# The value product of 8 of 12 column blocks through Strassen's seven quarter products, two of its four multiplications on GpSimd, in a new order

## The chip, the cores and the metric

The kernel runs on one core of one Trainium2 chip. The core has TensorE (PE: matmuls, and PEld, its weight loads), VectorE (DVE), ScalarE (ACT), GpSimd (POOL) and SyncE (SP), which here issues the DMAs. Each engine takes its instructions in the order of its own queue and waits on semaphores for the others. The metric is the device time of one execution in microseconds (us).

## The reference

The inputs are q, k and v (8 batches, 8 heads, 576 positions, head size 64) and three weights. First comes a retention layer, a causal attention whose scores are multiplied by a decay instead of going through a softmax; its output, 4608 tokens of 512 values, is x. Then comes a gated feed-forward layer of width 1536:

```python
ret = (q @ k.T / sqrt(64)) * Dmat          # Dmat[i, j] = gamma_h ** (i - j) for i >= j, else 0
x = (ret @ v) rearranged to (4608, 512)
gate = 1 / (1 + exp(-(x @ w_gate)))        # 512 x 1536
val = x @ w_val                            # 512 x 1536
out = (gate * val) @ w_out                 # 1536 x 512
```

Inputs and output are float32; the kernel's matmuls take bf16 and sum in float32.

## The kernel before, in words

**Blocks.** The tokens are taken in blocks of 512, 256, 384, 384 and then six of 512 (t0 = 1536 to 4096). While the feed-forward layer of one block runs, the retention layer makes the x of the next one: its steps ("slots", `slot_of_two`) are put between the pieces of the feed-forward work by the loop at the end of the kernel, so the order on every engine is written out by hand; no scheduler moves an instruction.

**Strassen.** In the 512-token blocks a 2-by-2 product of quarters is made from 7 quarter products instead of 8. The 12 column blocks (128 wide) of the gate make 3 units of 4 blocks; a unit is the product of a 2-by-2 arrangement of weight quarters (two halves of the 512 inner rows, two pairs of column blocks) and of x quarters (two halves of the inner rows, two halves of 256 tokens). One quarter product is `product`: 4 matmuls of 256 columns. A direct column block (`value`) is 4 matmuls of 512 columns. The step g16 is unit 1's product 6 of the gate, v4 the direct value product of column block 4. The sums of the weights (`wgt_sb`) are made once, in the blocks of 384 tokens; the sums of x (`xsum`) for each block by GpSimd.

**A gate unit's evictions.** The products gather in three PSUM banks, a, g and e. After product 1 ScalarE copies a to g; product 2 is added into g and ScalarE takes the sigmoid of g. After 6 ScalarE copies a to SBUF (u2), after 5 it copies e (s5). After 3 VectorE adds e to u2, after 7 it adds a to s5, and ScalarE takes the sigmoids of both; after 4 ScalarE takes that of a. The sigmoids go to `gv`. `settle` puts the last two sigmoids behind the matmuls of the following step. A direct value block is one VectorE multiplication, gv times the PSUM bank.

**Output part.** `quarters` makes gv @ w_out with Strassen again, from gv and its sums `gsum` (per unit: third_sum on GpSimd, the others on VectorE; for unit 2 all four on GpSimd, for each pair of column blocks). Between its products stand two retention slots in every 512-token block but the last. In a slot (`slot_of_two`) PE makes the values of two steps (`val`), VectorE then reads one element of each bank (`glance`), PE makes the scores and products of two new steps, and then the second part of `val`, which goes to the banks that glance has read. Products 1 and 2 of the next block's first gate unit (`gates_early`) stand at the end of the output part; the first 512-token block has no such place ahead of it and starts with g01 and g02.

**Order and room.** `ORDER` is the list of steps of a 512-token block, with the sums that stand behind a step after a colon. PSUM has eight banks: tr, pv and st one each, qk two, and a ring of three (`ffn_psum`). Finished output tiles wait in `stores` until more than KEEP are there, then the oldest leaves on SP's queue. GpSimd's other work is the casting of q, k and v (`casts_to`), which SP then transposes by DMA.

Of the kernel before, what the change touches and what calls it, by code (L numbers as in the profile page):

```python
# [16 lines left out]
def kernel(  # L17
# [32 lines left out]
    osb_pool = ctx.enter_context(tc.tile_pool(name="osb", bufs=13))  # L50
# [4 lines left out]
    sum_pool = ctx.enter_context(tc.tile_pool(name="sum", bufs=5))  # L55
# [26 lines left out]
    ffn_psum = Ring(3)  # L82

# [174 lines left out]
    sbd = [(consts if i else lead).tile([P, M, P], BF16, name=f"sbd{i}") for i in range(4)]  # L258
# [43 lines left out]
    wgt_sb = consts.tile([P, 3, NU, 2, 2 * P], BF16)  # L302

    def wg_quarters(u):

        fa, fb = (slice((4 * u + 2 * y) * P, (4 * u + 2 * y + 2) * P) for y in range(2))
        return wg_sb[:, 0:2, fa], wg_sb[:, 2:4, fa], wg_sb[:, 0:2, fb], wg_sb[:, 2:4, fb]

    def wg_sums(i, u):

        a11, a12, a21, a22 = wg_quarters(u)
        s1, s2, s4 = (wgt_sb[:, j, u] for j in range(3))
        to, a, b, op = ((s1, a21, a22, ALU.add), (s2, s1, a11, ALU.subtract), (a21, a11, a21, ALU.subtract),
                        (s4, a12, s2, ALU.subtract))[i]
        nc.vector.tensor_tensor(out=to, in0=a, in1=b, op=op)
# [202 lines left out]
    def third_out(apart):  # L518

        ps = pair_ps[5][0][0]  # L520
        share = nat_pool.tile([P, 2, P], FP32, tag="apart", name="apart", bufs=1)
        nc.vector.tensor_copy(out=share, in_=apart)
        cols = slice(5 * P, 6 * P)
        nc.vector.tensor_tensor(out=x_out(slice(0, 2), cols), in0=x_in(ps[:, 0:2], cols), in1=x_in(share, cols), op=ALU.add)
        nc.scalar.copy(out=x_out(slice(2, 4), cols), in_=x_in(ps[:, 2:4], cols))
# [188 lines left out]
    def leave_share(s, j):  # L714

        if before(s, j) is not None:
            shares[s, j] = nat_pool.tile([P, 2, 64], FP32, tag="share", name=f"share_{s}_{j}", bufs=4)
            nc.scalar.copy(out=shares[s, j], in_=val_ps[s][1 - j][:, M:M + 2])
# [140 lines left out]
    KEEP = 9  # L859
# [59 lines left out]
    def gate_units(gvs, t0):  # L919

        units = []
        banks = [(tr_psum, "tr", pv_psum, "pv", qk_psum, "qk"), (qk_psum, "qk", ffn_psum, "ffn", st_psum, "st"),
                 (pv_psum, "pv", st_psum, "st", tr_psum, "tr")]
# [6 lines left out]
        def bank(u, i, name):  # L930
            pool, tag = banks[u][2 * i:2 * i + 2]
            more = {"written": True} if pool is ffn_psum and name == "g" else {}
            return pool.tile([P, 2, 256], FP32, tag=tag, name=f"gate{name}_{t0}_{u}", **more)

        def keep(u, name, ps):
            t = sum_pool.tile([P, 2, 256], FP32, tag="sum", name=f"gate{name}_{t0}_{u}")
            nc.scalar.copy(out=t, in_=ps)
            return t
# [7 lines left out]
        def left(u, i):  # L946
            a11, a12, a21, a22 = wg_quarters(u)
            return (a11, a12, wgt_sb[:, 2, u], a22, wgt_sb[:, 0, u], wgt_sb[:, 1, u], a21)[i - 1]

        def product(u, i, ps, first):  # L950
            w, x = left(u, i), right(i)
            for f in range(2):
                for kc in range(2):
                    nc.tensor.matmul(ps[:, f], lhsT=w[:, kc, f * P:(f + 1) * P], rhs=x[:, kc],  # L954
                                     start=(first and f == 0 and kc == 0), stop=(f == 1 and kc == 1),
                                     skip_group_check=True)

        of = [{} for _ in range(NU)]

        def gate(u, i):  # L960

            me = of[u]
            if i == 1:
                gv_tile(gvs, t0, 4 * u)
                me["unit"] = made[t0, u]
                me["a"] = bank(u, 0, "a")
            if i == 5:
                me["e"] = bank(u, 2, "e")
            a, e = me["a"], me.get("e")
            product(u, i, {1: a, 6: a, 7: a, 4: a, 5: e, 3: e, 2: me.get("g")}[i], i in (1, 5))  # L970
            settle()

            def sigmoid(r, h, src):
                nc.scalar.activation(out=me["unit"][:, 2 * r:2 * r + 2, h * 256:(h + 1) * 256], in_=src, func=AF.Sigmoid)  # L974

            if i == 1:
                me["g"] = bank(u, 1, "g")
                nc.scalar.copy(out=me["g"], in_=a)
            elif i == 2:
                sigmoid(0, 0, me["g"])  # L980
            elif i == 5:
                me["s5"] = keep(u, "s5", e)
            elif i == 6:
                me["u2"] = keep(u, "u2", a)
            elif i == 3:
                nc.vector.tensor_tensor(out=me["u2"], in0=e, in1=me["u2"], op=ALU.add)  # L986
                waiting.append(lambda: sigmoid(0, 1, me["u2"]))
            elif i == 7:
                nc.vector.tensor_tensor(out=me["s5"], in0=a, in1=me["s5"], op=ALU.add)
                waiting.append(lambda: sigmoid(1, 1, me["s5"]))  # L990
            else:
                sigmoid(1, 0, a)
            return 4 * 256

        def value(fc):

            ps = ffn_psum.tile([P, 512], FP32, tag="ffn", name=f"h2_{t0}_{fc}")
            for kc in range(NKC):
# [6 lines left out]
        return gate, value  # L1005

    EARLY = "g01 g02"
    ORDER = ("g05 g06 g11 g03 g07 g12 g15 v0 g04 v1 g16 v2 g13 v3 g17 g21 v4:00 g14 v5:01:02 g22 g25 v6 g26 g23 v7 "
             "g27 v8 v9:10:2 g24 v10 v11:11:12:2")
    begun = {}  # L1010

    def gates_early(t0):

        gvs = {}
        gate, value = gate_units(gvs, t0)
        begun[t0] = gvs, gate, value
        for x in EARLY.split():
            yield gate(int(x[1]), int(x[2]))

    def quarters(gvs, sums, t0, k):  # L1020
# [42 lines left out]
        def keep(name, ps):  # L1063
            kept[name] = sum_pool.tile([P, 2, W], FP32, tag="sum", name=f"s{name}_{t0}")[:, 0:k]
# [91 lines left out]

    def ffn_units(t0, n, nxt):
        if n < 512:
# [3 lines left out]
            return  # L1162
        if t0 not in begun:
            for cols in gates_early(t0):
                yield cols
        gvs, gate, value = begun[t0]
        sums = []
        for x in ORDER.split():
            if x[0] == "g":
                yield gate(int(x[1]), int(x[2]))  # L1170
                continue
            x, *behind = x.split(":")
            fc = int(x[1:])
            cols = value(fc)
            u = fc // 4
            if fc % 4 == 0:
                sums.append(pair_sums(t0, u))
            if u < NU - 1 and fc % 4 == 3:
                third_sum(made[t0, u], sums[u], slice(0, 2))
            for one in behind:  # L1180
                if len(one) == 2:
                    gv_sum(made[t0, int(one[0])], sums[int(one[0])], slice(0, 2), int(one[1]), nc.vector)
                    continue
                pair = slice(fc % 4 // 2, fc % 4 // 2 + 1)
                for i in range(2):
                    gv_sum(made[t0, u], sums[u], pair, i, nc.gpsimd)
                third_sum(made[t0, u], sums[u], pair)
                gv_sum(made[t0, u], sums[u], pair, 2, nc.gpsimd)
# [225 lines left out]
    for w, (t0, n) in enumerate(BLOCKS):  # L1414
# [6 lines left out]
        if n == 512:  # L1421
            n_h = len(ORDER.split()) + (0 if t0 in begun else len(EARLY.split()))
# [11 lines left out]
        for i, cols in enumerate(ffn_units(t0, n, nxt)):  # L1434
            if w in (1, 2) and i % 2 == 0 and i < 18:
                which, part = (0, 1, 3)[i // 2 % 3], i // 6
                if w == 1:
                    wg_sums(which, part)
                else:
                    wo_sums(which, part, 3)  # L1440
            if w == 2 and n_h <= i < n_h + NU:
                wg_sums(2, i - n_h)
# [53 lines left out]
```

## Time and profile before

| | us |
|---|---|
| median of 3 runs | 317.99 (317.87 to 318.19) |
| the profiled execution | 318.03 |
| its span | 316.3 |
| PE busy | 307.6 |
| VectorE / ScalarE / GpSimd busy | 210.4 / 169.7 / 177.1 |
| gate-and-value part of a 512-token block (five of the six) | 18.89 to 18.90 |
| the same in the first, with g01 and g02 | 20.65 |

The profile is one execution. PE's rows overlap, since matmuls are pipelined: the distance from one row's start to the next one's is what a step costs. The "gate-and-value part" goes from the first product of `ORDER` (g05) to the first product of the output part (qa), read from TensorE's timeline.

### The profile page before, as it was taken

What the parts mean: (1) busy time and instruction counts of PE and PEld (TensorE: products, weight loads), DVE (VectorE), ACT (ScalarE), POOL (GpSimd) and SP (SyncE); (2) the same over time, 40 slices, a digit from 0 to 9 for tenths busy, and PEclk for the clock granted to TensorE, in tenths of its full rate; (3) what the DMA queues carried; (4) which work ended last, traced back from release to release, by engine and by line L of the source; (5) the groups of instructions that cost most, each with busy time, mean ns of one, the idle gap of its engine ahead of it and who ended that gap; (6) DMA issues with size and microseconds to landing.
All of it is one profiled execution on the core that took longest, in us unless ns stands there. A gap on an engine that the chain in (4) does not pass through costs nothing. (4 is left out here: it accounts for less than half of the span.)

```text
span 316.3 us, 9821 instructions
## 1 busy us (share of the span) xinstructions
PE 307.6 (97%) x4038; PEld 210.7 (67%) x4038; DVE 210.4 (67%) x478; ACT 169.7 (54%) x374; POOL 177.1 (56%) x238
## 2 busy tenths in 40 slices
PE   7999999999999998999999999999999999999994
PEld 6664557856545655668866786678667866786683
DVE  6955656778826775688568955885689558826843
ACT  6855555555434337554665476537654765446530
POOL 5784545544644834119981899189918921841170
PEclk9999999999999999999999999999999999999999
DMA  7999999998999999920589549944992167022004
GB/s 219 329 381 390 333 301 209 190 183 188 209 218 168 254 224 235 199 50 5 104 181 254 132 98 188 284 103 96 207 199 70 37 204 263 2 68 68 2 0 134
DMA packets 146045, 55.19 MB, mean 174 GB/s; under 512 B 125393, under 2 KB 137937, under 8 KB 146001
## 3 DMA queue, kind: packets, MB, share of 16 engines
q1 hardware_dynamic: 145200, 53.92, 71.8%
q10 hardware_dynamic: 800, 0.66, 0.7%
q8 instruction: 31, 0.51, 0.6%
q14 instruction: 14, 0.11, 0.1%
HBM read 37.75 MB, written 9.44 MB: 149 GB/s over the span
## 5 line engine op out<-in xcount | busy, mean ns | idle before, releaser
L999 PE MATMUL h<-xT,wv_sb 128*128 128x512 bf16 x288 | 72.0, 379 | 0.0
L1002 DVE TENSOR_TENSOR gv<-gv,h 128x512 bf16<-128x512 bf16 x72 | 49.5, 688 | 23.1 <-PE h L999 20.7
L892 POOL TENSOR_TENSOR gsum<-gv 128x512 bf16<-128x512 bf16 (+1 forms) x24 | 21.9, 913 | 55.7 <-DVE gv L1002 55.7
L375 POOL TENSOR_TENSOR qk<-k,ktab 128x512 bf16<-128x512 f32 x30 | 31.6, 1054 | 23.5 <-DMA k<-in_k_dram 16.5
L999 PEld LDWEIGHTS <-wv_sb 128*128 128x128 bf16 x288 | 28.2, 98 | 21.2
L954 PEld LDWEIGHTS <-wg_sb 128*128 128x128 bf16 x288 | 27.7, 98 | 13.2 <-issue 1.0
L375 POOL TENSOR_TENSOR qk<-q,qtab 128x512 bf16<-128x512 f32 x28 | 29.7, 1061 | 3.2 <-DMA q<-in_q_dram 3.1
L1053 PEld LDWEIGHTS <-gsum 128*128 128x128 bf16 x288 | 27.8, 98 | 3.4
L620 DVE TENSOR_TENSOR pt<-row,tri 128x256 bf16<-128x256 f32 x60 | 21.6, 418 | 12.6 <-PE row L613 10.9
L824 PE MATMUL h<-xT,wv_sb 128*128 128x384 bf16 (+1 forms) x144 | 26.8, 308 | 0.0
L824 PE MATMUL h<-xT,wg_sb 128*128 128x384 bf16 (+1 forms) x144 | 26.8, 308 | 0.0
L954 PEld LDWEIGHTS <-wgt_sb 128*128 128x128 bf16 x216 | 21.1, 98 | 7.0
L986 DVE TENSOR_TENSOR gateu<-gatee,gateu 128x512 f32<-128x512 f32 x18 | 12.4, 689 | 20.1 <-PE gatee L954 18.3
L581 ACT CAST sb<-s 128x256 bf16<-128x256 f32 x44 | 17.8, 408 | 9.4 <-DVE s L740 5.6
L1053 PEld LDWEIGHTS <-gv 128*128 128x128 bf16 x204 | 19.6, 98 | 3.7
L380 POOL CAST v<-v 128x512 bf16<-128x512 f32 x29 | 17.9, 617 | 7.1 <-DMA v<-in_v_dram 4.1
L1150 PE MATMUL op<-wo_sb,gv 128*128 128x512 bf16 x96 | 21.7, 379 | 0.0
L954 PE MATMUL gatea<-xsum,wg_sb 128*128 128x256 bf16 x144 | 21.6, 273 | 0.0
L838 ACT ACTIVATE gv<-h 128x384 bf16<-128x384 f32 x24 | 11.8, 491 | 18.1 <-PE h L824 18.0
L974 ACT ACTIVATE gv<-gateu 128x512 bf16<-128x512 f32 x18 | 11.3, 630 | 17.6 <-DVE gateu L986 17.6
L689 ACT CAST xT<-val 128x256 bf16<-128x256 f32 x46 | 13.9, 385 | 9.4 <-PE val L647 6.5
L824 PEld LDWEIGHTS <-wg_sb 128*128 128x128 bf16 x144 | 13.8, 98 | 7.3 <-DVE xT L728 0.2
(159 smaller groups left out, 643.4 us busy)
## 6 DMA issues: line engine op xcount, KB each, us to landing
k<-in_k_dram SPq DMA_DIRECT2D x26, 256.0 KB, 3.9
q<-in_q_dram SPq DMA_DIRECT2D x26, 256.0 KB, 4.3
v<-in_v_dram SPq DMA_DIRECT2D x26, 256.0 KB, 4.5
out_dram<-ob SPq DMA_DIRECT2D x25, 256.0 KB, 2.7
wg<-in_moe_w_gate_dram SPq DMA_DIRECT2D x12, 256.0 KB, 5.1
wv<-in_moe_w_val_dram SPq DMA_DIRECT2D x12, 256.0 KB, 5.2
wo<-in_moe_w_out_dram SPq DMA_DIRECT2D x12, 256.0 KB, 5.0
v32p<-in_v_dram SPq DMA_DIRECT2D x6, 256.0 KB, 4.7
```

The lines of the kernel that those rows point to most:

```text
L375: eng.tensor_tensor(out=natural_qk[s][:, i].rearrange("p m (y d) -> p y m d", y=2), in0=by_halves(loaded[s][1 - i]), in1=tab, op=ALU.mult)
L380: eng(out=natural["v", s], in_=loaded[s][2])
L581: eng(out=state[key], in_=src)
L620: nc.vector.tensor_tensor(out=probs[s][:, y], in0=row_ps[s][y][:, 0], in1=tri.unsqueeze(1).to_broadcast([P, M, 64]), op=ALU.mult)
L689: nc.scalar.copy(out=x_out(ALL, cols_of(s, i)), in_=x_in(val_ps[s][i], cols_of(s, i)))
L824: nc.tensor.matmul(out, lhsT=w_sb[:, kc, fc * P:(fc + 1) * P], rhs=xT(kc, slice(t0 + a, t0 + e)), start=(kc == 0), stop=(kc == NKC - 1))
L892: nc.gpsimd.tensor_tensor(out=s3, in0=a11, in1=a21, op=ALU.subtract)
L954: nc.tensor.matmul(ps[:, f], lhsT=w[:, kc, f * P:(f + 1) * P], rhs=x[:, kc], start=(first and f == 0 and kc == 0), stop=(f == 1 and kc == ...
L999: nc.tensor.matmul(ps, lhsT=wv_sb[:, kc, fc * P:(fc + 1) * P], rhs=xT(kc, slice(t0, t0 + 512)), start=(kc == 0), stop=(kc == NKC - 1))
L1002: nc.vector.tensor_tensor(out=gvs[fc], in0=gvs[fc], in1=ps, op=ALU.mult)
L1053: nc.tensor.matmul(ps[:, b], lhsT=left(fp)[:, b * P:(b + 1) * P], rhs=right(fp), start=(first and fp == 0 and b == 0), stop=(fp == NFC // ...
L1150: nc.tensor.matmul(opp, lhsT=gvs[fc][:, nb * P:(nb + 1) * P], rhs=wo_sb[:, fc, :], start=(fc == 0), stop=(fc == NFC - 1))
```

## The change

The columns of the value product are also grouped in units of four. Units 0 and 1 (column blocks 0 to 7) go through seven quarter products in the 512-token blocks; blocks 8 to 11 stay direct. A value unit is evicted as a gate unit is, but where the gate has a sigmoid the value has a multiplication into gv: the quarters from g and a on VectorE (both are in PSUM), those from u2 and s5 on GpSimd (both are in SBUF). The sums of the value's weights are eight GpSimd operations in the second block of 384 tokens. A steady block's list has 37 steps for 31. The order is new throughout; in the first 512-token block g05 and g11 come between g01 and g02. Behind v11 stand three VectorE sums (11, 02, 12) where two stood (11, 12). To make room the output tiles go from 13 to 11 and KEEP from 9 to 7, and some small tiles share the slots of the sums, seven for five.

```diff
-    osb_pool = ctx.enter_context(tc.tile_pool(name="osb", bufs=13))
+    osb_pool = ctx.enter_context(tc.tile_pool(name="osb", bufs=11))
-    sum_pool = ctx.enter_context(tc.tile_pool(name="sum", bufs=5))
+    sum_pool = ctx.enter_context(tc.tile_pool(name="sum", bufs=1))
...
+    SUMS = 7
+    sum_next = [0]
+
+    def sum_tile(shape, dt, name, slot=None, of=SUMS):
+        if slot is None:
+            slot = sum_next[0] % of
+            sum_next[0] += 1
+        return sum_pool.tile(shape, dt, tag=f"sum{slot}", name=name)
...
-    def wg_sums(i, u):
+    def w_sums(kind, i, u, eng):
...
-        nc.vector.tensor_tensor(out=to, in0=a, in1=b, op=op)
+        eng.tensor_tensor(out=to, in0=a, in1=b, op=op)
...
-            shares[s, j] = nat_pool.tile([P, 2, 64], FP32, tag="share", name=f"share_{s}_{j}", bufs=4)
+            shares[s, j] = sum_tile([P, 2, 256], FP32, f"share_{s}_{j}", of=4)[:, :, 0:64]
...
-    KEEP = 9
+    KEEP = 7
...
-        banks = [(tr_psum, "tr", pv_psum, "pv", qk_psum, "qk"), (qk_psum, "qk", ffn_psum, "ffn", st_psum, "st"),
-                 (pv_psum, "pv", st_psum, "st", tr_psum, "tr")]
+        BANKS = {("g", 0): [(tr_psum, "tr"), (pv_psum, "pv"), (qk_psum, "qk")],
+                 ("g", 1): [(qk_psum, "qk"), (ffn_psum, "ffn"), (st_psum, "st")],
+                 ("g", 2): [(pv_psum, "pv"), (st_psum, "st"), (tr_psum, "tr")],
+                 ("w", 0): [(ffn_psum, "ffn"), (qk_psum, "qk"), (ffn_psum, "ffn")],
+                 ("w", 1): [(ffn_psum, "ffn"), (ffn_psum, "ffn"), (ffn_psum, "ffn")]}
...
+            def leaves(r, h, src, eng=nc.vector):
+                to = made[t0, u][:, 2 * r:2 * r + 2, h * 256:(h + 1) * 256]
+                if kind == "g":
+                    nc.scalar.activation(out=to, in_=src, func=AF.Sigmoid)
+                else:
+                    eng.tensor_tensor(out=to, in0=to, in1=src, op=ALU.mult)
...
             elif i == 3:
                 nc.vector.tensor_tensor(out=me["u2"], in0=e, in1=me["u2"], op=ALU.add)
-                waiting.append(lambda: sigmoid(0, 1, me["u2"]))
+                waiting.append(lambda: leaves(0, 1, me["u2"], nc.gpsimd))
             elif i == 7:
                 nc.vector.tensor_tensor(out=me["s5"], in0=a, in1=me["s5"], op=ALU.add)
-                waiting.append(lambda: sigmoid(1, 1, me["s5"]))
+                waiting.append(lambda: leaves(1, 1, me["s5"], nc.gpsimd))
             else:
-                sigmoid(1, 0, a)
+                leaves(1, 0, a)
...
-            ps = ffn_psum.tile([P, 512], FP32, tag="ffn", name=f"h2_{t0}_{fc}")
+            pool, tag = (qk_psum, "qk") if fc < NFC - 2 else (ffn_psum, "ffn")
+            ps = pool.tile([P, 512], FP32, tag=tag, name=f"h2_{t0}_{fc}")
...
-    ORDER = ("g05 g06 g11 g03 g07 g12 g15 v0 g04 v1 g16 v2 g13 v3 g17 g21 v4:00 g14 v5:01:02 g22 g25 v6 g26 g23 v7 "
-             "g27 v8 v9:10:2 g24 v10 v11:11:12:2")
+    ORDER = ("w05 g03 w01 g15 g07 g16 g12 w06 g04 g13 g21 g17 w03 w11 w07 w02 g25 g26 w04 w12:00"
+             " w16 w15 g14:01 w17:0t g27 w13 g23 g22 w14:10:1t v8 g24 v9 v10 v11:11:02:2a:12:2b").split()
...
+    def steps_of(t0):
+        return ("g05 g06 g11" if t0 in begun else "g01 g05 g11 g02 g06").split() + ORDER
...
+            if w == 2 and i % 2 and i < 6 * NQ:
+                w_sums("w", (0, 1, 3)[i // 2 % 3], i // 6, nc.gpsimd)
...
+            if w == 2 and n_h + NU <= i < n_h + NU + NQ:
+                w_sums("w", 2, i - n_h - NU, nc.gpsimd)
```

A step wUI is product I of value unit U; 00, 01, 02, 0t, 2a after a colon are the sums of gv (unit, then which one; t the third on GpSimd, a and b the four of a pair of blocks on GpSimd).

## The prediction

> **What bounds the kernel now.** I read the page's busy times first, then the chain that ended last, then the timeline of TensorE, then the other queues where TensorE might have to wait.
>
> ```profile
> span 316.3 us, 9821 instructions
> ...
> PE 307.6 (97%) x4038; PEld 210.7 (67%) x4038; DVE 210.4 (67%) x478; ACT 169.7 (54%) x374; POOL 177.1 (56%) x238
> ```
> ```profile
> 286.43 0.44 PE gatee L954 x4
> 286.87 0.86 PE h L999 x4
> 287.73 0.44 PE gatea L954 x4
> ```
> TensorE is busy 97% of the span, and the chain is almost wholly PE. In the second fence each row is one step: a quarter product of four 256-column matmuls takes 0.44 us, a direct column block of four 512-column ones 0.86. Over longer stretches these are 0.4365 and 0.865: half the columns cost half the time, so fewer columns are fewer microseconds, provided PE doesn't start waiting.
>
> The timeline of the first 512-token block shows where it waits today, and ScalarE's in the third block how tightly its queue runs:
> ```profile
> 122.80 0.60 PE L954 MATMUL gatea<-xT,wg_sb 128*128 128x256 bf16 x4
> 124.18 0.60 PE L954 MATMUL gateg<-xT,wg_sb 128*128 128x256 bf16 x4 [0.78 <-ACT gateg L978]
> ...
> 125.49 0.60 PE L954 MATMUL gatea<-xT,wg_sb 128*128 128x256 bf16 x4
> 126.00 0.60 PE L954 MATMUL gatee<-xT,wgt_sb 128*128 128x256 bf16 x4
> ```
> ```profile
> 189.39 0.60 ACT L937 COPY gates<-gatee 128x512 f32<-128x512 f32 x1
> 189.86 0.63 ACT L937 COPY gateu<-gatea 128x512 f32<-128x512 f32 x1
> 190.34 0.64 ACT L978 COPY gateg<-gatea 128x512 f32<-128x512 f32 x1
> ```
> g01 to g02 takes 1.38 us instead of 0.44. ScalarE's evictions last 0.60 us, but start every 0.48. VectorE's (L986, L989, L1002: 0.69) start every 0.61.
>
> The table of windows gives the third block's gate-and-value part (second row) and the output part before it (first row); columns are PE, PEld, DVE, ACT, POOL busy.
> ```profile
> 175.78:188.61 12.83, 12.83 (x342) 11.35 (x341) 10.13 (x30) 7.53 (x20) 12.60 (x19) 1.00 0.37 84
> 188.61:207.50 18.89, 18.89 (x127) 12.04 (x124) 12.61 (x21) 11.42 (x22) 10.59 (x13) 1.00 1.03 240
> ```
> The granted clock is 1.00. In the gate-and-value part no other engine is above 12.61 of 18.89; in the output part GpSimd is full, 12.60 of 12.83. There VectorE and GpSimd meet (timeline, all engines):
> ```profile
> 208.31 0.43 DVE L898 TENSOR_TENSOR gsum<-gsum,gv 128x512 bf16<-128x512 bf16 x1
> 208.42 0.85 POOL L898 TENSOR_TENSOR gsum<-gv,gsum 128x256 bf16<-128x256 bf16 x1
> 208.84 0.71 DVE L898 TENSOR_TENSOR gsum<-gv,gsum 128x512 bf16<-128x512 bf16 x1
> 209.23 0.84 POOL L898 TENSOR_TENSOR gsum<-gv 128x256 bf16<-128x256 bf16 x1
> 209.58 0.23 DVE L675 COPY glance<-val 128x1 f32<-128x1 f32 x2
> ...
> 209.86 0.32 PE L647 MATMUL val<-T,sb 64*64 64x64 bf16 x16
> ```
> A sum with both inputs in SBUF takes 0.42 alone on VectorE; the second one here ends 0.28 after GpSimd's operation ended (209.27), and GpSimd's next ends 0.52 after VectorE's: they take turns. `glance` stands behind these sums in VectorE's queue, and PE's second batch of `val` matmuls waits for it: PE starts 0.28 after glance. So VectorE's lateness here is PE's, but for at most 0.11 (blocks 1, 2 and 4 start 0.38 after glance, since PE itself is still busy).
>
> **The change part by part.** The sum is against the profiled execution, 318.03 us (span 316.3 and 1.7 around it), 0.04 above the median 317.99.
>
> *Fewer columns, new order.* A steady block issues 19 products and 12 column blocks: 8.29 + 10.38 = 18.67; its window is 18.89, so 0.22 are stalls (g11 to g03 0.57 instead of 0.44, and two more of 0.05), which go where g03 moves two steps further from the eviction it waits for. After: 33 products and 4 blocks, 14.40 + 3.46 = 17.86. To see whether PE then waits I walk the new queues from g05 = 0, with the pitches above, an eviction ready 0.64 after its product's start, and 0.05 from an eviction's end to PE:
> - ScalarE, 24 operations before the last column blocks: ws5 copy at 2.22; sigmoid of u2 at 3.12 (VectorE's add 2.39 to 3.08); copy of w01 3.69 to 4.27, wanted by w06 at 4.37: slack 0.05. Then each in turn: u2 of gate unit 1 ends 5.8 (g17 at 6.12), w06's copy 6.8 (w07 at 7.43), w11's copy 9.35 (w12 at 9.61), w16's 11.28 (w17 at 11.36). All hold, barely.
> - VectorE: w04's multiplication is ready at 9.82 and ends 10.51; w15 wants that bank at 10.49: 0.07 stall. The rest is in time (w17's add ends 12.7, for w14 at 13.6). v11's multiplication ends 0.9 after the output part begins, as today.
> - GpSimd: its casts end 7.3 to 7.5 after g05 (195.84 in block three), and wu2 is ready at 8.06. The mixed bf16-by-f32 multiplication isn't in the trace: its rows lie between L375's 1.05 and L892's 1.16. I take 1.1, by L375, whose form (f32 in, bf16 out) is nearest. The first two end by 10.3; VectorE's gsum needs the second at 11.04. Cover 0.8, so these four cost nothing; if they came over 0.8 late, VectorE's queue behind gsum (ws5's add, which w14 waits for, 0.8 early) would follow. Gsum itself meets GpSimd's third sum (10.3 to 11.4) and can be 0.4 late, inside that slack.
>
> Window 17.93, against 18.89: 0.96 in five blocks, 4.8 us. The first: 20.65 now, of which 1.1 are stalls; after, g05 and g11 stand between g01 and g02, so 35 products and 4 blocks, 18.74 and 0.1: 1.8; what is late next there is w15, as elsewhere. Together **-6.6**.
>
> The "GPSIMD Engine Reference" of the Trainium skill (4.1 Engine selection) speaks against part of this: two-input elementwise work belongs on VectorE, GpSimd being about twice slower. Twice L1002's 0.69 would make an estimated 1.38 each, the second ending at 10.9, still before 11.04; by that rule the sum stays as it is.
>
> *A third sum before glance.* Unit 0's fourth sum now stands behind v11 too, so three sums instead of two go ahead of glance, all beside GpSimd's eight. Bounds: none (VectorE runs them on end, 3 x 0.38, no later than today), and 1.1 (each of three waits for a GpSimd operation, the first too). I take one more blocked sum, 0.71 and a 0.03 gap, the row that is nearest: 0.74, less the slack 0.11 in three blocks: 3 x 0.63 + 2 x 0.74 = **+3.4** in five blocks (0 to 5.5). The last block has no glance.
>
> The Trainium skill's page "SBUF — State Buffer" (Who interferes with whom) says that the second to issue is blocked until the first has finished its whole instruction. By that the first sum, arriving 0.2 into a GpSimd sum, waits as well, 1.1 a block, and this term would be 5.0 to 5.5; the rows show the first unblocked in five blocks of five, and I keep 3.4.
>
> *End of the last block.* Product 6 reads unit 2's second sum at 306.0; GpSimd has it at 305.67. It starts 0.5 later against PE (it waits for v9's multiplication, which the late sigmoids of unit 2 hold) and loses 0.4 to VectorE's extra sum: 0.9 - 0.35 = **+0.5** (0 to 0.9).
>
> *Weight sums in the 384-token block.* Six GpSimd sums (1.16 each) between 96 and 106, beside VectorE's eight w_out sums (L299, 0.42 alone, 0.62 to 0.85 where GpSimd is at work). VectorE has hardly a gap there until 102; a value bank is wanted 1.95 after its product starts and is free 1.35 after, so 0.6 of lateness is hidden. **+0.3** (0 to 1.5). The two later ones stand behind GpSimd's v cast at 113.6. GpSimd's casts for steps 11 to 15, and the transposes and loads that SP has queued behind them, move by about 3.5; those transposes are first read at 119 and 145, 12 us and more after: nothing.
>
> *Nothing:* two output buffers fewer and KEEP 7 for 9 (a store still leaves with each new one, the buffer reused was sent a block earlier); the shared slots (the tightest, ws5 of unit 1, is free at 10.3 and written at 11.2); memory for sbd, shares, apart.
>
> Sum: -6.6 + 3.4 + 0.5 + 0.3 = -2.4: 318.03 - 2.4 = **315.6 us**.
>
> **The rivals.**
> - *The three sums run on end.* For it: nothing shows that GpSimd can step between sums that don't depend on each other. Against: it does so between the two of today. 315.6 - 3.4 = 312.2; with the other two costs at their bounds 311.4 to 313.8.
> - *ScalarE becomes the bound* (slower). Place: the chain of 24 evictions, where w06, w12 and w17 have 0.05, 0.2 and 0.03 of slack. The four rows from PSUM show 0.48; those fed from SBUF (L974 from gateu) 0.54 to 0.59. If the mean is 0.61 (as their durations) instead of 0.5, the 16 up to w11's copy lose 1.7 less 0.2: 1.5 in six blocks, 9 us: 324. It decides from 2.4 / 6 = 0.4 a block, a mean pitch 0.04 above mine.
> - *GpSimd's multiplications are late*: beyond 1.6 together w14 waits one for one; at 2.0 each instead of 1.1, 0.2 to 1 a block: 317 to 321. Nothing in the rows of L375 and L892 speaks for it.
> - That the column count doesn't fall is excluded: the changed queues hold 144 more matmul pairs, 12 units x (28 - 16).
>
> **How the numbers follow.** My case, 313.7 to 317.5 (glance 0.3 to 1.1 a block, the other two costs as taken): 0.50. Sums on end: 0.27. ScalarE: 0.13. GpSimd late: 0.05. Something unseen that makes it slower: 0.05. 0.2%, 0.64 us, is about what can be told from no change. Faster 0.77, same 0.05, slower 0.18. The range leaves out the best bounds of the second case and the slow cases: 311.6 to 318.2.
>
> **What would show it.** Gate-and-value windows of 17.9 to 18.1 (18.8 to 18.9 in the first), no row of PE idle at g02; w15 the only regular wait. Glance 2.8 after the output part's start instead of 2.06, with PE's val idle before it by DVE glance; if glance is at 2.1, the second case. PE idle by ACT at w06, w12 or w17 would show the third. The prediction is wrong if a queue that I walked with steady pitches has a wait that I placed before its need: ScalarE's above all.

## The result, and the profile after

The changed kernel takes 320.18 us (319.6 to 320.5), the kernel before 317.99 (317.87 to 318.19): 1.0066 times as long, with a 95% interval of 1.0048 to 1.0084. The forecast was 315.6 and a gain. The time lies outside the range and on the other side.

The profiled execution of the changed kernel took 320.48 us, 2.45 more than the one of before. Its page begins:

```profile
span 318.8 us, 10201 instructions
...
PE 303.6 (95%) x4165; PEld 225.4 (71%) x4182; DVE 219.3 (69%) x478; ACT 184.7 (58%) x410; POOL 216.7 (68%) x270
```

TensorE is busy 4.0 us less (303.6 instead of 307.6), and yet the span grew by 2.5: 6.5 us more of it are idle. The table of windows for the third block (the output part before it, then its gate-and-value part) answers to the table that the prediction showed:

```profile
178.51:192.44 13.93, 13.20 (x342) 11.52 (x340) 11.01 (x31) 7.49 (x20) 13.62 (x20) 1.00 0.46 96
192.44:210.44 18.00, 17.95 (x150) 14.45 (x148) 12.58 (x20) 13.92 (x28) 14.55 (x16) 1.00 1.03 237
```

The second row is what the change was made for: 18.00 instead of 18.89, with PE (the second number, 17.95) as good as always busy. The first row is the output part, 13.93 instead of 12.83, with 0.73 of PE idle.

The whole way through the kernel, read from TensorE's timeline, adds up as follows.

| stage (us) | before | after | difference |
|---|---|---|---|
| first h product of the 384-token blocks | 70.26 | 70.78 | +0.52 |
| from there to the first gate product of the 512-token blocks | 52.54 | 57.38 | **+4.84** |
| first gate-and-value part | 20.65 | 18.89 | -1.76 |
| the five others together | 94.46 | 89.99 | -4.47 |
| five output parts together | 64.39 | 67.66 | **+3.27** |
| last output part, to the first matmul of qf | 7.86 | 8.42 | +0.56 |
| start of qf (sum of the rows above) | 310.16 | 313.12 | +2.96 |
| from there to the end of the span | 6.15 | 5.65 | -0.50 |

The first row is start-up: PE waited a little longer for the first weights, which also differs between executions of one kernel (70.81 and 71.69 in two profiles of the same kernel further down). The last row was not forecast, and no run was made on it; it is 5.6 to 5.8 in every run with the new order.

The largest new loss is in a stage where no product changed. The description of the kernel gives the sums of x (`xsum`) to GpSimd; that holds for five of the six 512-token blocks, but those of the first are made by VectorE, in both kernels, and they matter here. This is the timeline of the changed kernel (rows of VectorE, GpSimd, ScalarE and PE) at the end of the second 384-token block; the columns are start, duration, engine and line, operation, output<-inputs, and in brackets the idle time before it and what ended it:

```profile
116.85 2.63 POOL L328 TENSOR_TENSOR wv_sb<-wv_sb 128x512 bf16<-128x512 bf16 x2
...
118.46 1.17 DVE L930 TENSOR_TENSOR xsum<-xT 128x256 bf16<-128x256 bf16 x1
119.44 1.08 POOL L388 TENSOR_TENSOR qk<-k,ktab 128x512 bf16<-128x512 f32 x1
...
119.66 1.02 DVE L930 TENSOR_TENSOR xsum<-xT,xsum 128x256 bf16<-128x256 bf16 x1
...
120.49 1.08 POOL L388 TENSOR_TENSOR qk<-q,qtab 128x512 bf16<-128x512 f32 x1
120.60 1.12 DVE L930 TENSOR_TENSOR xsum<-xT 128x256 bf16<-128x256 bf16 x1
121.52 0.67 POOL L393 CAST v<-v 128x512 bf16<-128x512 f32 x1
121.64 0.69 DVE L930 TENSOR_TENSOR xsum<-xT,xsum 128x256 bf16<-128x256 bf16 x1
...
122.26 0.93 DVE L753 TENSOR_TENSOR s<-s,row 128x256 f32<-128x256 f32 x2
...
122.70 0.93 ACT L594 CAST sb<-s 128x256 bf16<-128x256 f32 x2 [3.67 <-DVE s L753]
123.16 0.25 PE L660 MATMUL val<-T,sb 64*64 64x64 bf16 x6 [2.58 <-ACT sb L594]
```

And this is the same place in the kernel before:

```profile
114.20 1.04 POOL L375 TENSOR_TENSOR qk<-k,ktab 128x512 bf16<-128x512 f32 x1
115.20 1.04 POOL L375 TENSOR_TENSOR qk<-q,qtab 128x512 bf16<-128x512 f32 x1
...
117.56 0.29 DVE L917 TENSOR_TENSOR xsum<-xT 128x256 bf16<-128x256 bf16 x1
117.88 0.29 DVE L917 TENSOR_TENSOR xsum<-xT,xsum 128x256 bf16<-128x256 bf16 x1
118.09 0.28 DVE L917 TENSOR_TENSOR xsum<-xT 128x256 bf16<-128x256 bf16 x1
118.29 0.28 DVE L917 TENSOR_TENSOR xsum<-xT,xsum 128x256 bf16<-128x256 bf16 x1
118.49 0.94 DVE L740 TENSOR_TENSOR s<-s,row 128x256 f32<-128x256 f32 x2
...
119.01 0.61 POOL L380 CAST v<-v 128x512 bf16<-128x512 f32 x1 [2.77 <-DMA v<-in_v_dram]
...
119.39 0.25 PE L647 MATMUL val<-T,sb 64*64 64x64 bf16 x6 [0.26 <-ACT sb L581]
```

Before, the four sums of x take 0.28 each: GpSimd happens to be idle just then (2.77 before its cast at 119.01). After, GpSimd's casts of k and q, which before were done by 116.24, start at 119.44 and 120.49; GpSimd runs without a gap, and each of VectorE's four sums ends 0.15 after one GpSimd operation has ended: 4.0 us instead of 1.1 for the four. `s` stands behind them on VectorE, ScalarE's cast of s to `sb` waits for that, and PE waits 2.58 us for the cast.

The clock then fell. The windows 121 to 125 and 125 to 128.16 of the changed kernel (the last columns are the granted clock, DMA share and GB/s):

```profile
121.00:125.00 4.00, 1.51 (x72) 1.23 (x74) 3.56 (x10) 2.08 (x6) 3.23 (x4) 0.84 1.25 198
125.00:128.16 3.16, 3.16 (x11) 1.20 (x10) 2.59 (x10) 0.82 (x3) 0.61 (x1) 0.66 1.11 285
```

The two numbers are means: within these windows the clock stands at 0.50 from 123.7 to 127.1 and at 1.00 on both sides. From that val row to the first gate product it is 5.00 us after and 3.41 before, for the same work: 1.59 more. So the +4.84 are 2.3 of PE's wait, 1.6 of clock, and 0.9 in small delays earlier (the largest at 103.02, an idle time of 0.40, where VectorE's `gv` was late beside the first six weight sums).

The drop is no accident of the profiled execution. The mean granted clock over the whole span is recorded for every timed execution, and it is 0.992 to 0.994 in all four of the changed kernel. It is 0.995 or less in 23 of the 43 executions of the kernels whose profile shows a wait of 1.6 to 3.0 us at this place (the changed one and four of the runs below), and in 1 of the 109 of all others, among them 60 of the kernel before.

The loss in the output parts is the one that was forecast. VectorE and GpSimd in the changed kernel's output part of the first 512-token block:

```profile
147.41 0.67 POOL L911 TENSOR_TENSOR gsum<-gsum,gv 128x256 bf16<-128x256 bf16 x1
147.85 0.50 DVE L911 TENSOR_TENSOR gsum<-gsum,gv 128x512 bf16<-128x512 bf16 x1
148.04 0.85 POOL L905 TENSOR_TENSOR gsum<-gv 128x256 bf16<-128x256 bf16 x1
148.28 1.69 DVE L911 TENSOR_TENSOR gsum<-gv,gsum 128x512 bf16<-128x512 bf16 x2
...
148.85 0.84 POOL L911 TENSOR_TENSOR gsum<-gv,gsum 128x256 bf16<-128x256 bf16 x1
...
149.66 0.84 POOL L911 TENSOR_TENSOR gsum<-gv 128x256 bf16<-128x256 bf16 x1
149.90 0.21 DVE L688 COPY glance<-val 128x1 f32<-128x1 f32 x2
...
150.16 0.26 PE L660 MATMUL val<-T,sb 64*64 64x64 bf16 x8 [0.50 <-DVE glance L688]
```

The first of the three sums takes 0.50, the other two 0.85 each, `glance` comes 2.85 after the output part's start, and PE waits for it. From the first output product (qa) to the third (qe) it is 3.36 or 3.37 in all five blocks, where it was 2.56 to 2.71.

### The profile page after: what moved, and what is told of

Read it like the earlier page. It is cut to its first block, busy times and chain, and to the rows that moved or that the text cites. A ratio compares the mean times of both kernels' runs of the same rounds, so it can differ in the third digit from the quotient of the medians.

```text
span 318.8 us, 10201 instructions
## 1 busy us (share of the span) xinstructions
PE 303.6 (95%) x4165; PEld 225.4 (71%) x4182; DVE 219.3 (69%) x478; ACT 184.7 (58%) x410; POOL 216.7 (68%) x270
## 5 line engine op out<-in xcount | busy, mean ns | idle before, releaser
L994 POOL TENSOR_TENSOR gv<-gv,wu 128x512 bf16<-128x512 bf16 x12 | 14.0, 1165 | 28.5 <-DVE wu L1006 28.3
L1006 DVE TENSOR_TENSOR gu<-gatee,gu 128x512 f32<-128x512 f32 x18 | 12.4, 688 | 29.2 <-ACT gateg L998 16.9
L905 POOL TENSOR_TENSOR gsum<-gv 128x512 bf16<-128x512 bf16 (+1 forms) x24 | 24.3, 1012 | 2.4 <-DVE gv L994 1.8
L971 PEld LDWEIGHTS <-wgt 128*128 128x128 bf16 x216 | 21.1, 98 | 2.5
L1020 PE MATMUL h<-xT,wv_sb 128*128 128x512 bf16 x90 | 21.4, 379 | 0.3
L971 PEld LDWEIGHTS <-wv_sb 128*128 128x128 bf16 x192 | 18.8, 98 | 2.2
L994 POOL TENSOR_TENSOR gv<-gv,ws 128x512 bf16<-128x512 bf16 x12 | 14.0, 1165 | 8.5 <-DVE ws L1009 8.5
```

Of the source, the lines that this page charges most:

```text
L905: nc.gpsimd.tensor_tensor(out=s3, in0=a11, in1=a21, op=ALU.subtract)
L994: eng.tensor_tensor(out=to, in0=to, in1=src, op=ALU.mult)
L1020: nc.tensor.matmul(ps, lhsT=wv_sb[:, kc, fc * P:(fc + 1) * P], rhs=xT(kc, slice(t0, t0 + 512)), start=(kc == 0), stop=(kc == NKC - 1))
```

## The experiments

### Moving the weight sums

The theory: the loss before the 512-token blocks comes from the eight weight sums on GpSimd (six between 96 and 107, two in place at 116.85), which meet VectorE there. The first run moves both groups, the next two move one each.

```diff
-            if w == 2 and i % 2 and i < 6 * NQ:
+            if w == 1 and i % 2 and i < 6 * NQ:
                 w_sums("w", (0, 1, 3)[i // 2 % 3], i // 6, nc.gpsimd)
...
-            if w == 2 and n_h + NU <= i < n_h + NU + NQ:
-                w_sums("w", 2, i - n_h - NU, nc.gpsimd)
+            if w == 3 and i in (1, 3):
+                w_sums("w", 2, i // 2, nc.gpsimd)
```

> The six GpSimd sums of the value's weights go from the second 384-token block to the first, the two sums in place into the first steps of the first 512-token block. Theory: they made GpSimd's casts late, the casts met VectorE's x sums at 118 to 122, and PE waited 2.6 us there and lost more at a lower clock: the first 512-token block begins 4 to 5 us earlier than in the changed kernel, 315.0 to 316.0. Rival, that the loss lies in the new order of the 512-token blocks: no more than 0.5 gained, 319.5 or more. Rival, that it is the sums themselves wherever they stand: they collide with the gate's weight sums on VectorE in the first 384-token block, and 1 to 3 us of loss move there: 317 to 319.

> Only the six sums move, the two in place stay. Theory: the casts are no longer 3 us late, but the two sums in place (2.6 us) still stand ahead of three casts, so some of VectorE's x sums are still blocked: 1 to 2 us of the 4.9 stay, 316 to 317.5. If the six alone made the loss: as with all eight moved, 315.0 to 316.0; if the two alone: 319 or more.

> Only the two sums in place move. Theory: the six still make the casts some 3 us late, but the casts end 2.6 us earlier; 2 to 3 us gained, 317 to 318.5. If the two in place alone made the loss: 315.0 to 316.0; if the six alone: 319 or more.

| | from the first h of the 384-token blocks to the first gate product | PE's wait at val | time | ratio to the kernel before |
|---|---|---|---|---|
| before | 52.54 | 0.26 | 317.99 | |
| changed | 57.38 | 2.58 | 320.18 | 1.0066 (1.0048 to 1.0084) |
| six sums moved | 54.52 | 1.58 | 319.28 | 1.0029 (0.9998 to 1.0060) |
| two in-place sums moved | 54.72 | 1.71 | 320.14 | 1.0028 (1.0010 to 1.0047) |
| all eight moved | 53.22 | 0.15 | 317.54 | 0.9957 (0.9933 to 0.9982) |

The ratios are to be compared, not the times: beside the last three rows the kernel before took 318.83. The second and third columns come from one profiled execution each; the times of the run with six sums moved spread from 317.28 to 321.52.

Moving all eight takes 4.16 of the 4.84 us away and turns the change into a gain. Either group alone leaves a wait of 1.6 to 1.7.

The times missed what was expected in all three runs, by 0.8 because the kernel before was slower by that much beside them, too. By its time the run with all eight moved lies where the third rival put it (317 to 319), and that rival has a part of the truth: 0.68 of the loss is left, most of it beside the sums' new place (PE idle 0.44 at 85.16, by DVE gv). The rest of the miss lies elsewhere: an idle time of 1.10 in the second output part, of the kind that the last experiment is about, where the changed kernel has 0.23. The other two times, 319.28 and 320.14, are those that were written down for "the other group alone"; the stages say that both groups count, 2.86 and 2.66 of the 4.84 taken away by moving one, and that they overlap. With all moved, the four sums of x are short again, because GpSimd is idle for 2.88 around them:

```profile
119.25 0.28 DVE L930 TENSOR_TENSOR xsum<-xT 128x256 bf16<-128x256 bf16 x1
119.56 0.29 DVE L930 TENSOR_TENSOR xsum<-xT,xsum 128x256 bf16<-128x256 bf16 x1
119.78 0.28 DVE L930 TENSOR_TENSOR xsum<-xT 128x256 bf16<-128x256 bf16 x1
119.98 0.28 DVE L930 TENSOR_TENSOR xsum<-xT,xsum 128x256 bf16<-128x256 bf16 x1
...
120.81 0.61 POOL L393 CAST v<-v 128x512 bf16<-128x512 f32 x1 [2.88 <-PE val L644]
121.08 0.25 PE L660 MATMUL val<-T,sb 64*64 64x64 bf16 x6 [0.15 <-ACT sb L594]
```

The run with the two in-place sums alone moved gained only 0.4% by the ratio: its first gate-and-value part took 20.36 instead of 18.89. The two sums stood beside three sums of w_out on VectorE (L310), the add behind these came late, and the value product w06 waited 1.32 for ScalarE's copy of wg. It is the same chain at another place. With all eight moved the same two sums met two of the next sums of x instead (1.13 and 1.24 each), and PE did not wait.

### Taking the third sum away from glance

```diff
-             " ... v10 v11:11:02:2a:12:2b").split()
+             " ... v10 v11:11:2a:2b").split()
...
+            if i in (4, 5):
+                gv_sum(made[t0, i - 4], sums[i - 4], slice(0, 2), 2, nc.vector)
```

The sums 02 and 12 are issued behind two later products of the output part; everything else is the changed kernel.

> Both VectorE sums that only the sixth product of the output part reads (the fourth sums of units 0 and 1) go behind the second product, so one sum stands ahead of glance instead of three. Theory: PE starts its second batch of val matmuls 0.65 us earlier in five blocks, and the last block's product 6 waits less: 3.3 + 0.4 gained, 316.2 to 316.9. Rival, that glance is late because v11's multiplication or GpSimd's multiplications are late: under 1 us gained, 319.2 or more. Rival, that the two sums now hold up the eviction ahead of product 5 instead: the gain is given back, 318.5 to 320.

One sum is left before `glance`, and PE has no wait there (timeline of the second block's output part in this run):

```profile
177.80 0.51 DVE L911 TENSOR_TENSOR gsum<-gsum,gv 128x512 bf16<-128x512 bf16 x1
...
179.05 0.22 DVE L688 COPY glance<-val 128x1 f32<-128x1 f32 x2 [0.74 <-PE val L660]
...
179.43 0.34 PE L660 MATMUL val<-T,sb 64*64 64x64 bf16 x16
```

`glance` now waits for PE instead of PE for it. From qa to qe it is 2.71, 2.71, 2.61, 2.71 and 2.56: to 0.01 the kernel before in every block. The edit takes two sums away from there, and the stage is then that of the kernel before, where two stood; so the price of the third sum is the difference between the two kernels, 0.65 to 0.80 a block, 3.5 in all. The time is 318.17, ratio 0.9969 (0.9937 to 1.0001), less gained than expected: the second output part has two idle times without a wait (0.55 and 1.10; the last experiment), and the last output part, where 0.4 was expected, stayed at 8.53.

### Which engine's lateness it is

In the next runs, all whose labels begin with c, the 28 DMA transposes of q and k are plain DMA copies of the same tiles:

```diff
-        nc.sync.dma_start_transpose(out=t.rearrange("p j m t -> p (j m) t"),
+        nc.sync.dma_start(out=t.rearrange("p j m t -> p (j m) t"),
```

This leaves the transposes out, so the retention layer works on untransposed q and k; the compute engines' instructions are the same. Two runs give the base: the kernel before and the changed kernel with nothing but this edit.

> The kernel before with its 28 DMA transposes of q and k replaced by plain DMA copies of the same tiles. Left out: the transposes, so the retention layer works on untransposed q and k; every instruction on the compute engines is as before. It is the base that the runs c_... are compared with. If the transposes' traffic (70% of the DMA engines' time) is what stalls PE here, as its issue stall of 0.42 in the first output part may be, that stall is gone; otherwise the stages are those of the kernel before to 0.1: block start 122.8 to 124, windows 20.65 and 18.89, qa to qe 2.56 to 2.71.

> The changed kernel with the same replacement (the 28 DMA transposes as plain copies). Theory (the losses lie with VectorE and GpSimd meeting at the SBUF, not with the DMA): start of the first 512-token block 4 to 5.5 later than in c_before, windows 18.89 and 18.00, qa to qe 3.36. Rival (the losses came through late DMA transposes, moved 3.5 later): the start is within 1.5 of c_before, since copies are short. The PE issue stall in the second output part (0.23 to 1.10 with transposes): 0 if it is instruction loading behind the transposes' traffic.

The kernel before with copies takes 318.61, ratio 1.0011 (0.9985 to 1.0036) to the real kernel before, as all ratios from here on; the changed one 320.4, ratio 1.0044 (1.0018 to 1.0071). Behind the start-up (70.70 and 72.87) all stages are those of the real kernels within 0.3, but for the stretch through the 384-token blocks: 52.86 and 56.40, so +3.54 where 4 to 5.5 was expected, with a wait at val of 2.99. The loss does not come through late transposes. It is smaller than 4.84 mainly because the clock stayed at 1.00 in this execution: from the val row to the first gate product it was again 3.41.

The next run tells GpSimd's lateness from VectorE's. GpSimd gets four operations more in the critical stretch, and VectorE four fewer:

```diff
         at = (col - t0) // 256
+        if t0 == 1536 and at == 0:
+            eng = nc.gpsimd
         if len([x for x in ready[t0] if (x - t0) // 256 == at]) < 2:
```

> c_after, its weight sums left where they are, but the four sums of x of the first 512-token block's first 256 tokens (xsum, 118.46 to 122.3 in the changed kernel's profile) made by GpSimd instead of VectorE. GpSimd has then even more to do there and its casts come later still. Theory (VectorE lost its time by having those four sums blocked behind one GpSimd operation each, and the state sum behind them held ScalarE's cast and PE): the state sum comes right behind VectorE's weight sums, PE's val wait at that place (2.58 in the changed kernel) falls under 0.7 and the block begins 2.5 to 4 earlier than in c_after. Rival (GpSimd's lateness by itself is what PE waits for, through its late casts): PE's wait stays at 2 or grows, start no earlier than c_after's.

```profile
117.81 0.42 DVE L328 TENSOR_TENSOR wg_sb<-wg_sb 128x512 bf16<-128x512 bf16 x1
...
118.14 0.94 DVE L753 TENSOR_TENSOR s<-s,row 128x256 f32<-128x256 f32 x2
...
118.40 0.67 POOL L932 TENSOR_TENSOR xsum<-xT 128x256 bf16<-128x256 bf16 x1 [1.57 <-ACT xT L702]
119.14 0.67 POOL L932 TENSOR_TENSOR xsum<-xT,xsum 128x256 bf16<-128x256 bf16 x1
119.77 0.67 POOL L932 TENSOR_TENSOR xsum<-xT 128x256 bf16<-128x256 bf16 x1
...
120.09 0.23 PE L660 MATMUL val<-T,sb 64*64 64x64 bf16 x8
...
120.28 0.24 PE L660 MATMUL val<-T,sb 64*64 64x64 bf16 x8
```

`s` comes straight behind VectorE's weight sums, and PE's wait is gone altogether. The stretch is 52.87, as with the kernel before (52.86), although the weight sums are where the change put them and GpSimd's next casts come nearly 5 us later still against the work (qk at 123.26, 7.7 after the op row at 115.52; with copies alone 3.1 after it). So VectorE's blocked sums were what PE waited for. What is late next showed as well: the next four sums of x and three of w_out met GpSimd, the add behind them was late, PE waited 1.90 for ScalarE's copy of wg, and the first gate-and-value part took 20.94. The time is 318.33, ratio 0.9988 (0.9968 to 1.0008).

### Both repairs

The weight sums moved, and the sums 02 and 12 put later:

> c_after with both repairs at once: the eight weight sums moved to the first 384-token block and to the first two slots of the first 512-token block, and unit 0's fourth sum put behind the first output products. Theory (the two losses lie at different places, have nothing to do with each other, and the stage gains stand as forecast): windows 18.89 and 18.00, qa to qe 2.56 to 2.71, block start 0.7 later than c_before without start-up differences: -1.76 - 4.5 + 0.7 + 0.6 = -5.0 against c_before, ratio to it 0.982 to 0.987; against c_after -7 to -8. Rival (the two repairs buy the same time twice): -3 to -4.5 against c_after.

314.13 us (313.18 to 315.29), ratio 0.9860 (0.9820 to 0.9899): 4.5 less than the kernel before with copies, where 5.0 was expected, and 6.3 less than the changed kernel with copies, where 7 to 8 was. Windows 18.89 and 18.00, qa to qe 2.56 to 2.71, the stretch through the 384-token blocks 52.50. The repairs add up.

> The same kernel as c_both, beside the next three on the same chip, as their base. 314.1 within 1.0, windows and output parts as in c_both, the issue stall of about 1.06 at the same matmul of the second output part (row 5055 of PE's instructions, the tenth of the second slot's last twelve val matmuls).

The second time it took 314.44, ratio 0.9850 (0.9813 to 0.9888). The stretch was 54.43 in the profiled execution, with waits of 0.61 and 0.39 for VectorE's `gv` at 84.86 and 88.20, beside the six sums at their new place. So these are not free there: 0 to 2 us, by the execution.

Both repairs together were run only with copies in place of the transposes. With transposes each was run alone: moving the sums is faster than the kernel before (0.9957), and the interval of the other (0.9969) just reaches 1.

### GpSimd's share, and the first block's order

Two parts of the change undone, on top of both repairs.

```diff
-                waiting.append(lambda: leaves(0, 1, me["u2"], nc.gpsimd))
+                waiting.append(lambda: leaves(0, 1, me["u2"]))
...
-                waiting.append(lambda: leaves(1, 1, me["s5"], nc.gpsimd))
+                waiting.append(lambda: leaves(1, 1, me["s5"]))
```

> c_both, and all four multiplications of a value unit on VectorE instead of two on GpSimd. Theory A (GpSimd's share is needed): VectorE, which runs with hardly a gap from 7 us after g05 on, gets 4 x 0.42 to 0.69 = 1.7 to 2.8 more in each window; PE waits 0.3 to 1.5 a block for banks, or in the output part for gv: 2 to 9 longer than c_both_again. Rival B (the share only buys back what it costs, since GpSimd's multiplications hold up VectorE's gsum): within 0.6 of c_both_again, windows 18.0 to 18.1.

323.94, ratio 1.0162 (1.0123 to 1.0202): 9.5 more than with the two multiplications on GpSimd, a little beyond theory A's range. The windows are 20.37, 19.90 and then 19.48 to 19.51, and in each PE waits twice for VectorE where a value bank has to come free, 0.45 and 0.60, the larger wait being this one (block three):

```profile
208.16 1.89 PE L1020 MATMUL h<-xT,wv_sb 128*128 128x512 bf16 x8 [0.60 <-DVE gv L994]
```

So with this order of steps GpSimd's share is what makes the gain possible; an order laid out for VectorE alone was not run. GpSimd's multiplications take 1165 ns each (group of L994 on POOL in the changed kernel), against 692 and 729 for the same two on VectorE in this run.

```diff
-        return ("g05 g06 g11" if t0 in begun else "g01 g05 g11 g02 g06").split() + ORDER
+        return ("g05 g06 g11" if t0 in begun else "g01 g02 g05 g06 g11").split() + ORDER
```

> c_both, and in the first 512-token block g02 again straight behind g01 (g01 g02 g05 g06 g11). Forecast's step (of the first block's 1.8 some 0.9 is g02's wait for ScalarE's copy, hidden by g05 and g11): PE idle 0.78 before gateg at g02, first window 18.89 + 0.8 to 0.95 = 19.7 to 19.85, all other windows as they are. Rival (the wait only moves to a later step): first window 18.89 to 19.1.

The first window is 19.76, with 0.73 of idle before g02's gateg by ScalarE, and the others are unchanged; 315.3, ratio 0.9873 (0.9833 to 0.9913). The order of the first block is worth 0.87, as the forecast had it.

### The stall that no wait explains

In 12 of the 14 profiled executions PE stood idle in an output part without waiting for anything the trace shows ("issue"). The kernel before, then both repairs with copies:

```profile
151.92 0.22 PE L647 MATMUL val<-T,sb 64*64 64x64 bf16 x3 [0.42 <-issue]
```
```profile
182.14 0.22 PE L660 MATMUL val<-T,sb 64*64 64x64 bf16 x3 [1.06 <-issue]
```

Counted in PE's program, matmuls and weight loads together, these are instructions 4031 and 5055, which is 1024 apart; a second stall of 0.55, in the run with the fourth sums late, was at 4799, 256 before the latter. A test with 60 instructions fewer at the very start (10 wide warm-up matmuls for 40 narrow ones, the same 4 us):

```diff
-    fill(10, 4)
+    fill(10)
```

> c_both with the 40 narrow warm-up matmuls at the very start replaced by 10 of four times the width: the same 4 us of PE, 60 instructions fewer in PE's program, nothing else. Theory (PE's issue stalls are the loading of its instructions in pieces of 256: the page shows 32 packets of 16 KB on the instruction queue, and the stalls stand at rows 4031, 4799 and 5055 of PE's program, a multiple of 256 apart): the piece now ends 60 rows later in the work, at row 5055 of the new order, the last of the four gatea matmuls (g01), and the 256 rows before it hold some 75 rows more of slow 256-column matmuls than before, about 4 us of work instead of 2.8; the stall of 1.06 leaves the val matmuls and is gone or under 0.3: second output part 12.8 to 13.1 instead of 14.1, time 0.8 to 1.3 less than c_both_again. Rival (the stall belongs to that place in the work, not to the count of instructions): it stays at the same val matmul, output part 14.1.

```profile
150.92 1.14 PE L1073 MATMUL qa<-wo_sb,gsum 128*128 128x256 bf16 x9 [0.72 <-issue]
```

The second block's output part is 12.83 instead of 13.81 to 14.11: the stall left that place. But a new one of 0.72 came in the first block's output part, before the fourth matmul of a qa product. This is instruction 4031 again, where the kernel before has its stall, at other work; with both repairs and all warm-up matmuls there was none at 4031. The stall follows the count of instructions, as expected; that it would be gone was wrong. The time is 312.68 against 314.44, ratio 0.9810 (0.9777 to 0.9842) against 0.9850 (0.9813 to 0.9888), whose intervals overlap.

## Why the prediction was wrong, step by step

**The step that failed** is "weight sums in the 384-token block": +0.3 (0 to 1.5) was put down, +4.84 stood in the profiled execution, and 3.1 and 3.5 in executions where the clock did not fall (55.68 against 52.54 in the run with the fourth sums late, 56.40 against 52.86 with copies). It failed in its last sentence. I followed GpSimd's casts, taken as 3.5 later, only through what they produce, the transposes first read at 119 and 145, and called the delay nothing. The casts also occupy GpSimd. They came 5.2 to 5.5 later, the two at 114.20 and 115.20 at 119.44 and 120.49, and there they stood beside VectorE's four sums of x, which before lay in a gap of GpSimd's. VectorE made these four in 4.0 us instead of 1.1, and PE waited 2.58 instead of 0.26 for what follows them. The run with these sums on GpSimd shows that this, and not the casts' results, was the cost. The upper end of the range for the step was worked out at the six sums' own place, where VectorE's lateness is indeed partly hidden, and not where the moved work ended up.

**The clock** was taken as 1.00 throughout. In the profiled execution the wait of 2.58 was followed by 3.4 us at half clock, 1.6 us lost, and the clocks of the changed kernel's other three executions are as low. No step of the forecast had a wait that long, so none priced it.

**Fewer columns, new order** was right in mechanism and size: -6.6 forecast, -6.23 measured (-1.76 and -4.47). The steady window is 18.00 for a forecast 17.93, the first 18.89 for 18.85. The walk through the queues held: no idle time of PE of 0.2 or more in the third block's window, and none by ScalarE at w06, w12 or w17; w15, forecast 0.07 late, was 0.14 late. GpSimd's multiplication is 1165 ns for an assumed 1.1. The Trainium skill, "GPSIMD Engine Reference" (4.1 Engine selection), gives about twice VectorE's time, from which I estimated 1.38; here it is 1.6 to 1.7 times VectorE's 692 and 729, and keeping all four on VectorE, as the page advises, cost 9.5 us with both repairs in place.

**A third sum before glance** was right in size: 0.63 and 0.74 a block forecast, 0.65 to 0.80 measured, undone completely by the edit that moves two of the three. One reading behind it was wrong. I took the first sum as unblocked, and as arriving 0.2 into a GpSimd sum. The GpSimd row just ahead of the prediction's fence on these sums is this one (kernel before, third block):

```profile
207.79 0.67 POOL L892 TENSOR_TENSOR gsum<-gv 128x256 bf16<-128x256 bf16 x1
```

The first sum, at 208.31, starts 0.52 into it and ends 0.28 after it, just as the second ends 0.28 after the next one: it waits too, but only 0.15 of the GpSimd sum is left, so it loses next to nothing. In the changed kernel 0.22 is left, and it takes 0.50. That it comes so late in GpSimd's sum is luck as far as the forecast goes; by the same rows it would have cost an estimated 0.4 more a block at the start of that sum. In sum, +3.4 was forecast for the five blocks against +3.52 from qa to qe (3.27 for whole output parts, in which the stalls by "issue" differ too).

**End of the last block**: +0.5 forecast, +0.56 measured, with PE waiting 0.38 for GpSimd's gsum. **Nothing** for buffers, KEEP and slots: no wait for them appeared.

**The rivals**: three sums run on end, no. ScalarE as the bound, no. GpSimd late, no. The slower outcome came from the 0.05 that was kept for something unseen. The sum without the failed step was -2.7, and it measures -2.2 to -2.4 (-6.23 + 3.27 + 0.56, or with 3.52); one term turned it round. The start-up's +0.52 and the end's -0.50 cancel.

## What to carry to other kernels

When work is added to an engine in front of other work, follow the displaced instructions to where they end up and look at what they run beside there, not only at who reads their results. VectorE's sums of x took 0.28 where GpSimd was idle and 0.69 to 1.17 beside it, so a gap of GpSimd's can be a resource that another engine's queue lives on. Work done once, outside the loop that a change is meant for, can be moved freely, and its place deserves the same walk as the loop: here it decided the sign.

## What the runs showed of the hardware

- A VectorE sum with two SBUF inputs that started while a GpSimd operation was running ended a fixed time after that operation: 0.15 us for `xsum` (128x256: 0.28 alone, 0.69 to 1.17 beside GpSimd at the end of the 384-token blocks), 0.28 us for `gsum` (128x512: 0.42 alone, 0.43 to 0.89 beside GpSimd in the output parts). So it loses what is left of the GpSimd operation when it starts, less about 0.15; where less than that was left, `gsum` took its 0.42. The Trainium skill, "SBUF — State Buffer" (Who interferes with whom), says that a VectorE instruction with two SBUF inputs contends with a GpSimd instruction that reads SBUF, and that the shared ports are an exclusive lock. The rows agree, for GpSimd's casts as well as its sums; in the prediction I had weighed it for `glance` and at the six sums' own place, not for the sums of x.
- The granted clock stood at 0.50 for 3.4 us after a wait of PE of 2.58 us in one profiled execution, and stayed at 1.00 after waits of 2.46 and 2.99 at the same place in two others. Over all executions of kernels whose profile shows a wait of 1.6 to 3.0 there, the mean clock is 0.995 or less in 23 of 43; which ones it hits stays open. The Trainium skill, "TensorE: Matmul & The Clock Gate" (Why this matters for your kernels), names gaps over about 3 us as the danger; here a shorter one was followed by a drop and a longer one was not. Its remark that the activity window is free-running (Part 1) would fit that, but these runs do not show it.
- PE's stalls by "issue" stand on a grid of its instruction count. Instructions 4031, 4799 and 5055 are a multiple of 256 apart, and with 60 instructions fewer ahead a stall stood at 4031 again, under different work. The page lists 31 packets with 0.51 MB on the instruction queue before and 32 with 0.52 MB after. The Trainium skill, "Runtime: NRT & Kernel Launch" (Instruction fetch mechanics), says that instructions come in blocks of 256 and that the crossing is mostly hidden. If the stalls are such crossings, which fits the grid but is not shown directly, single ones cost 0.23 to 1.10 us here, all in output parts, most of them where a retention slot uses up some 240 short instructions in about 1.5 us. Copies in place of the transposes did not remove them (1.06), so the transposes are not needed for them. Why one crossing stalls and another does not stays open.
